# Which engine copies, how one weight is prepared, and when TensorE's work counts as ready, in a kernel of causal attention and a maxout layer

## Chip, cores and metric

The kernel runs on one core of a Trainium2 chip. The metric is the time of one execution in microseconds (us), taken on the device; lower is better.

## What is computed

```python
def _attn_ref(q, k, v):                    # (8, 8, 576, 64) float32
    scores = np.matmul(q, k.transpose(0, 1, 3, 2)) / np.sqrt(64)
    block = np.arange(576) // 64
    scores = np.where(block[:, None] >= block[None, :], scores, -1e9)
    scores = scores - np.max(scores, axis=-1, keepdims=True)
    attn = np.exp(scores)
    attn = attn / (np.sum(attn, axis=-1, keepdims=True) + 1e-09)
    return np.matmul(attn, v)

def _moe_ref(x, w1, w2, w3, w_out):        # w1..w3 (512, 768), w_out (768, 512)
    h = np.maximum(np.maximum(x @ w1, x @ w2), x @ w3)
    return h @ w_out

# out = _moe_ref(heads of the attention side by side: (4608, 512), w1, w2, w3, w_out)
```

Eight batches of eight heads, causal by blocks of 64 rows, and behind them, for each of the 4608 rows, the largest of three products and one more product.

## The kernel before

**Tiling.** Two heads of 64 make a pair, which fills 128 partitions; a batch has four pairs (`hp` 0 to 3). Of the 576 rows of a pair, 512 are worked in tiles of 128 queries, and the last 64 rows of both heads together as one tile more (`qk4`, `p4`). Products are taken in float32 accuracy from two parts of each number, a high one and a low one: high x high, high x low, low x high, which makes three matmuls of each product (a triplet).

**Stages of a pair.** Load K, Q, V; turn K and Q so that the head's 64 numbers lie on partitions; scores into banks of PSUM named `sb` (`qk` L1138 for batch 0, `block` L1020 for the whole pairs of later batches, `qk4` L1146 and L1150); row maximum on VectorE (L491), exponential on ScalarE (L675, P), sums, a scaling of P; P is turned; P times V on TensorE (`pv` L1212); the output is split into high and low parts (`xh`, `xl`).

**Batch 0 is done in a different way.** It is cut into the first 256 rows of all four pairs (FRONT) and the other 320 (BACK, `part.last`). K, Q and P are turned here by TensorE's transposes into `sb` banks (`raise_qk` L936 and L940, `raise4` L945 and L948, `raise_p` L631), from which ScalarE (L284) or VectorE (L286) copies them (`place_qk` for K and Q into `kq`; `place4` and `place` for P into `pt` or `pz`). For later batches VectorE turns 32x32 pieces and transfers put them in place.

**The layer.** Its work of the batch before stands between the attention steps on TensorE: `product` (L1381, into banks `pm`), the maximum (L1395), `project` (L1410).

**Weights.** The four matrices come in 24 units of 128x512. The units are prepared between 20 and 130 us: ScalarE takes an absolute value and the high part, VectorE has five steps (L379 to L401), and the remainder goes to TensorE, which adds it up in a `pm` bank for ScalarE to copy. [...]

**What sets the order.** Each step is a `Job` with a rank, costs on the engines that may do it, and what it needs. `in_order` plays the program with these costs: an engine that is free takes the ready job of the lowest rank whose buffers are free. Each engine's instructions are then issued in the order that comes out. A job that can go to ScalarE or VectorE goes to the one that is free first. Buffers count as slots: five `sb` banks, three `pm` banks, two tiles each of `pt` and `pz`. A job for TensorE whose last need was met by another engine (or by a transfer) counts as ready some time after that in the plan, if its rank is over 100 (from about 105 us on); a wait for a slot gets no such addition. At the start small matmuls without use (`spin`, L1444) keep TensorE at work.

Of the kernel before, what the change touches and what calls it, by code (L numbers as in the profile page):

```python
# [64 lines left out]
def in_order(jobs, slots):  # L65


    free = {}
    busy = {e: False for e in LAG}
    until = {"DVE": 0.0, "POOL": 0.0}  # L70
    ready = {e: [] for e in LAG}
    events, seq, out = [], 0, []
    moving = 0.0

    def post(t, kind, job, eng=None):
        nonlocal seq
        seq += 1
        heapq.heappush(events, (t, seq, kind, job, eng))

    def arrive(t, job, by=None):  # L80
        for e in job.cost:
            late = 250.0 if e == "PE" and by and by != "PE" and job.rank > 100.0 else 0.0
            post(t + late + (LAG[by][e] if by else 0.0), "ready", job, e)
        if not job.cost:
            post(landing(t, job), "done", job, "SP" if job.lasts else by)

    def landing(t, job):

        nonlocal moving
        t1 = t + job.lasts  # L90
        if job.moved:
            moving = max(moving, t) + job.moved
            t1 = max(t1, moving + DMA)
        return t1

    for n, job in enumerate(jobs):
        job.n, job.begun = n, False
        if job.left == 0:
            arrive(0.0, job)
    while events:  # L100
        t = events[0][0]
        while events and events[0][0] <= t:
            _, _, kind, job, eng = heapq.heappop(events)
            if kind == "ready":
                heapq.heappush(ready[eng], (job.rank, job.n))
            elif kind == "idle":
                busy[eng] = False
                for nxt in job.soon:
                    nxt.left -= 1
                    if nxt.left == 0:  # L110
                        arrive(t, nxt, eng)
            else:
                for s in job.give:
                    free[s] = free.get(s, slots[s]) + 1
                for nxt in job.next:
                    nxt.left -= 1
                    if nxt.left == 0:
                        arrive(t, nxt, eng)
        for eng, queue in ready.items():
            if busy[eng]:  # L120
                continue
            later = []
            while queue:
                top = heapq.heappop(queue)
                job = jobs[top[1]]
                if job.begun:
                    continue
                if all(free.get(s, slots[s]) >= job.take.count(s) for s in job.take):
                    for s in job.take:
                        free[s] = free.get(s, slots[s]) - 1  # L130
                    job.begun = busy[eng] = True
                    out.append((job, eng))
                    took = job.cost[eng]
                    if eng in job.alone:

                        took += max(0.0, until["POOL" if eng == "DVE" else "DVE"] - t)
                        until[eng] = t + took
                    post(t + took, "idle", job, eng)
                    post(max(t + took, landing(t, job)), "done", job, eng)
                    break  # L140
                later.append(top)
            for top in later:
                heapq.heappush(queue, top)
    assert all(j.begun or not j.cost for j in jobs), "no order"
    if DEBUG:
        print("model end", t, {e: sum(j.cost[g] for j, g in out if g == e) for e in LAG})
    return out
# [11 lines left out]
def act(n, psum=True):  # L159
    return (55.0 if psum else 95.0) + n / 1.2  # L160
# [7 lines left out]
def kernel(  # L168
# [30 lines left out]

    SECOND = 9  # L200
    NEAR = 4
    APART = 13
    XB = 3
    END = 40
    SPINS = 20
# [67 lines left out]

    def job(cost, rank, call, *args, after=(), take=(), give=(), lasts=0.0, moved=0.0, behind=None, alone=("POOL",)):
        j = Job(cost, rank, lambda eng: call(eng, *args), after, take, give, lasts, moved, behind, alone)
        jobs.append(j)
        return j

# [234 lines left out]
    class Head:  # L513
# [64 lines left out]
        def plain_turns(self, t0):  # L578
            pair, part = self.pair, self.pair.part
            heads = pair.heads  # L580
            shared = part.loads == 1 and self.j
            gate = heads[0].gate if shared else None
            first = heads[0].placed[0] if shared else None
            self.placed = []

            def place(call, *args, n, after):
                j = job(
                    {"ACT": act(n), "DVE": dve(n)} if part.last or pair.hp < 2 else {"ACT": act(n)},
                    t0 + 12,
                    call,  # L590
                    *args,
                    after=(after, first or (self.placed[0] if self.placed else None)),
                )
                self.placed.append(j)
                return j

            if part.last:
                if not self.j:
                    up = job({"PE": 4 * RAISE}, t0 + 11, pair.raise4, 0, after=(pair.scaled,), take=("sb", pair.tag, pair.tag))
                    pair.up4 = up, job({"PE": RAISE}, t0 + 11, pair.raise4, 1, after=(up,), take=("sb",))  # L600
                    join(pair.up4, ("p4",))
                gate = self.gate = pair.up4[0]
                for a, n in ((0, 256), (1, 64)):
                    place(self.place4, a, n=n, after=pair.up4[a])
                    if self.j:
                        join((self.placed[a], heads[0].placed[a]), ("sb",))

            for ts in [(t,) for t in part.tiles] if part.last else [part.tiles]:
                n = sum(ts) + len(ts)
                up = job(  # L610
                    {"PE": RAISE * n},
                    t0 + 12,
                    self.raise_p,
                    ts,
                    after=(*(self.scales[t] for t in ts), gate),
                    take=("sb",) if gate else ("sb", pair.tag),
                )
                gate = self.gate = gate or up
                join((up,), tuple(f"p{t}" for t in ts))
                join((place(self.place, ts, n=P * n, after=up),), ("sb",))  # L620
            self.moved = join(self.placed, ())
            self.first = None
            return None
# [92 lines left out]
    class Pair:  # L716
# [181 lines left out]
        def plain_qk(self, rank, loads):  # L898

            part, o = self.part, self.at // P  # L900
            banks = ((range(4), ((0, 0, 256),)),)
            if not self.apart:
                banks = (((o, o + 1, 4 + o, 5 + o), ((0, 1, 256), (256, 2, 256))),)
            if part.last:
                banks = ((2, 3, 8), ((0, 1, 256), (256, 0, 64))), ((4, 5, 6, 7), ((0, 2, 512),))
            ups, downs = [], []
            for n, (chunks, copies) in enumerate(banks):
                up = job(
                    {"PE": (2 * RAISE if self.apart else RAISE) * len(chunks)},
                    rank,  # L910
                    self.raise_qk,
                    n,
                    chunks,
                    after=(loads["kn"], loads["qn"]),
                    take=("sb", "sb5") + (("kq",) if n == 0 else ()),
                ) if n == 0 else job(
                    {"PE": RAISE * len(chunks)}, rank, self.raise_qk, n, chunks, after=(ups[0], loads["kn"], loads["qn"]), take=("sb", "sb5")
                )
                ups.append(up)
                put = []  # L920
                for c0, which, w in copies:
                    m = w if which else 2 * w
                    both = {"ACT": act(m), "DVE": dve(m)}
                    if not part.last:
                        both = {e: both[e] for e in (("ACT",) if which < 2 else ("DVE",))}
                    put.append(job(both, rank + 1, self.place_qk, n, c0, which, w, after=(up, *downs[:1]) if part.last else (up,)))
                    downs.append(put[-1])
                join(put, ("sb", "sb5"))
            join(ups, ("kn", "qn") * part.loads if not self.apart else (self.apart,))
            return join(downs, ())  # L930
# [588 lines left out]
```

## Time and profile before

| | us |
|---|---|
| Median of 3 runs (lowest to highest) | 859.13 (858.63 to 859.31) |
| The profiled execution's own time | 858.44 |
| Span of that execution in the trace | 856.7 |

| Engine | Busy, us | Share of span |
|---|---|---|
| TensorE, matmuls | 847.1 | 99% |
| TensorE, weight loads | 673.7 | 79% |
| VectorE | 521.0 | 61% |
| ScalarE | 467.4 | 55% |
| GpSimd | 292.6 | 34% |

The profiled execution took 1.74 us more than its span, and 0.69 us less than the median. PE is TensorE's matmuls, PEld its loading of weights (which runs beside them), DVE VectorE, ACT ScalarE, POOL GpSimd. Rows of a timeline give the start in us from the span's start, the time taken, and in brackets how long the engine was idle before and what ended it. Rows of one kind that follow each other are drawn together: `x20` is twenty instructions, and the time is from the first's start to the last's end, so a wait inside such a run lengthens it and doesn't appear as idle time.

### The profile page before, as it was taken

How to read it: one execution, taken by the hardware profiler on the slowest of the kernel's cores; microseconds unless marked ns; L12 is line 12 of the kernel's file. 1: busy time of each engine (PE TensorE's matmuls, PEld its weight loads, DVE VectorE, ACT ScalarE, POOL GpSimd, SP SyncE). 2: the span in 40 equal slices, each digit the busy share in tenths (PEclk: the TensorE clock that was granted, in tenths of full speed). 3: DMA queues.
4: the chain of work that ended last, by engine and by line, in shares of the span. 5: the costliest groups of instructions: out<-in, count | busy, mean ns of one | idle time of the engine just before them, and what ended most of it. 6: DMA issues, size and time to landing. Idle time of an engine off the chain costs nothing.

```text
span 856.7 us, 14921 instructions
## 1 busy us (share of the span) xinstructions
PE 847.1 (99%) x4866; PEld 673.7 (79%) x4866; DVE 521.0 (61%) x1540; ACT 467.4 (55%) x1305; POOL 292.6 (34%) x339
## 2 busy tenths in 40 slices
PE   8999999999999999999999999999999999999997
PEld 6677877788877788788878887888788778888886
DVE  6999998868782876568664866386638710110110
ACT  6997777667772765546573657465665422111111
POOL 3321113554453354514461345234443323110110
PEclk9999999999999999999999999999999999999999
DMA  8765348785777366745583558455655441001002
GB/s 239 216 191 142 69 96 190 140 186 100 164 162 171 62 138 146 160 105 112 111 191 77 112 117 180 110 120 121 132 143 108 93 116 63 0 1 50 0 1 50
DMA packets 240974, 100.36 MB, mean 117 GB/s; under 512 B 203008, under 2 KB 232704, under 8 KB 240896
## 3 DMA queue, kind: packets, MB, share of 16 engines
q1 hardware_dynamic: 236272, 86.42, 46.4%
q0 software_dynamic: 3456, 12.58, 4.6%
q8 instruction: 39, 0.64, 0.3%
q10 hardware_dynamic: 1168, 0.39, 0.2%
q14 instruction: 39, 0.32, 0.1%
HBM read 42.99 MB, written 10.49 MB: 62 GB/s over the span
## 4 chain that ended last, share of the span: by engine, by line
PE 91%; DVE 4%; ACT 3%; issue 1%; DMA 1%; SPq 0%; POOL 0%; ACTq 0%; DVEq 0%
PE pm L1381 51%; PE pm L1410 16%; PE pm L1212 7%; PE sb L1020 6%; PE sb L1150 2%; PE sb L1212 2%; ACT p L675 1%; DVE pz L698 1%; PE pm L414 1%; PE sb L1138 1%; DVE sb L491 1%; PE sb L631 1%; PE sb L1146 1%; PE sb L936 1%; PE pm L416 0%
## 5 line engine op out<-in xcount | busy, mean ns | idle before, releaser
L1381 PE MATMUL pm<-xh,w 128*128 128x512 f32 (+1 forms) x1296 | 386.4, 371 | 0.0
L1381 PEld LDWEIGHTS pm<-xh,w 128*128 128x128 f32 x1296 | 237.3, 188 | 45.1 <-issue 5.2
L1381 PE MATMUL pm<-xl,w 128*128 128x512 f32 (+1 forms) x648 | 237.3, 366 | 0.0
L675 ACT ACTIVATE p<-sb,nm 128x128 f32<-128x128 f32 (+3 forms) x256 | 133.7, 529 | 97.3 <-DVE nm L491 94.4
L1395 DVE TENSOR_TENSOR m<-pm,m 128x512 f32<-128x512 f32 (+1 forms) x120 | 74.5, 621 | 138.7 <-PE pm L1381 138.1
L698 DVE STREAM_TRANSPOSE pz<-p 128x512 f32<-128x512 f32 x280 | 133.6, 522 | 25.4 <-POOL p L511 11.3
L289 POOL TENSOR_TENSOR hl<-m,hh 128x512 fp32r<-128x512 f32 (+1 forms) x60 | 71.8, 1196 | 220.3 <-ACT hh L284 212.0
L491 DVE CUSTOM_DVE_ANT_1 sb<-sb,mask 128x256 f32<-128x256 f32 (+2 forms) x224 | 120.5, 566 | 37.0 <-PE sb L1150 34.9
L1381 PEld LDWEIGHTS pm<-xl,w 128*128 128x128 f32 x648 | 122.2, 189 | 19.2 <-issue 1.0
L1410 PE MATMUL pm<-wo,hh 128*128 128x512 f32 x432 | 134.1, 392 | 0.0
L289 POOL TENSOR_TENSOR kq<-kq 128x576 fp32r<-128x576 f32 x48 | 68.3, 1430 | 158.4 <-ACT kq L284 158.4
L511 POOL TENSOR_TENSOR p<-p,rs 128x512 f32<-128x512 f32 (+4 forms) x97 | 80.3, 853 | 101.8 <-DVE rs L852 65.2
L284 ACT CAST hh<-m 128x512 fp32r<-128x512 f32 (+1 forms) x60 | 34.6, 577 | 132.3 <-DVE m L1395 132.2
L284 ACT COPY m<-pm 128x512 f32<-128x512 f32 (+1 forms) x96 | 53.6, 559 | 93.2 <-PE pm L1410 63.5
L507 ACT ACTIVATE p<-p,rs 128x128 f32<-128x128 f32 (+4 forms) x176 | 89.3, 567 | 11.7 <-DVE rs L852 7.5
L1410 PEld LDWEIGHTS pm<-wo,hh 128*128 128x128 f32 x432 | 80.1, 188 | 16.8 <-issue 0.3
L1410 PE MATMUL pm<-wo,hl 128*128 128x512 f32 x216 | 84.2, 390 | 0.0
L1212 PE MATMUL pm<-pt,vn 128*64 128x320 f32 (+4 forms) x616 | 64.4, 360 | 0.0
L1212 PEld LDWEIGHTS pm<-pt,vn 128*64 128x64 f32 x616 | 38.5, 137 | 24.5 <-issue 1.4
L1020 PEld LDWEIGHTS sb<-kq 64*128 64x128 f32 x576 | 47.9, 185 | 8.7 <-issue 7.1
L1020 PE MATMUL sb<-kq 64*128 64x256 f32 (+3 forms) x576 | 53.1, 326 | 0.0
L675 ACT ACTIVATION_READ_ACCUMULATOR p<-sb,nm 128x1 f32 x256 | 51.5, 201 | 0.0
(129 smaller groups left out, 964.6 us busy)
## 6 DMA issues: line engine op xcount, KB each, us to landing
pt<-pz SPq DMA_DIRECT2D x224, 200.0 KB, 3.8
w<-in_moe_w_dram POOLq DMA_DIRECT2D x18, 512.0 KB, 5.5
vn<-in_v_dram SPq DMA_DIRECT2D x64, 128.0 KB, 3.5
out_dram<-m SPq DMA_DIRECT2D x32, 256.0 KB, 2.0
kq<-in_k_dram SPq DMA_DIRECT2D x112, 72.0 KB, 2.5
kq<-in_q_dram SPq DMA_DIRECT2D x112, 72.0 KB, 2.5
wo<-in_moe_w_out_dram POOLq DMA_DIRECT2D x6, 512.0 KB, 4.0
kq<-in_k_dram SPq DMA_DIRECT2D x8, 128.0 KB, 5.1
```

What stands on the lines that cost most here:

```text
L284: nc.scalar.copy(dst, src)
L289: {"DVE": nc.vector, "POOL": nc.gpsimd}[eng].tensor_tensor(out=dst, in0=a, in1=b, op=ALU.subtract)
L491: nc.vector.tensor_tensor_reduce(out=ps, in0=ps, in1=hidden, scale=-SCALE, scalar=first, op0=ALU.add, op1=ALU.min, accum_out=out_)
L507: nc.scalar.mul(p, p, r)
L511: nc.gpsimd.tensor_tensor(out=p, in0=p, in1=r.broadcast_to([P, p.shape[1]]), op=ALU.mult)
L675: nc.scalar.activation(dst, src, AF.Exp, bias=nm[:, c : c + 1], scale=-1.0, accum_out=sm[:, c : c + 1])
L698: nc.vector.transpose(dst, p[:, 0 : n * P])
L1020: nc.tensor.matmul(h.ps[t], qs[h.own, P * t : P * (t + 1)], ks[h.own, 0 : P * (t + 1)], start=(n == 0), stop=(n == 2),)
L1212: nc.tensor.matmul(o[h.own].rearrange("p (i u) -> p i u", u=n)[:, :, c0 : c0 + z - a], self.vn[own, kt, h.j, :], h.pt[own, :, h.off + a : ...
L1381: nc.tensor.matmul(self.ps, w[i, f][:, c, :], xx, start=(c == 0 and s == 0), stop=(c == NC - 1 and s == 2))
L1395: nc.vector.tensor_tensor(out=m, in0=ps, in1=m, op=ALU.max)
L1410: nc.tensor.matmul(self.po, h, w[f], start=(f == 0 and s == 0), stop=(f == NF - 1 and s == 2))
```

## The change

Five edits.

1. The time that TensorE's jobs count as ready later was 250 (ns in the plan) for all; now it is 700 for jobs `qk4`, `block` and `pv`, and 250 for the others.
2. `APART` is 12 instead of 13: unit number 12 (`w12`) has its remainder made by VectorE and takes two matmuls instead of three.
3. Turned P of BACK's pairs 2 and 3 is copied by ScalarE alone.
4. K and Q of BACK's pairs 2 and 3 are copied by ScalarE alone.
5. K and Q of FRONT's first two pairs are copied by one VectorE copy of 2x256 columns, instead of a ScalarE copy of 256 and a VectorE copy of 256.

```diff
     def arrive(t, job, by=None):
         for e in job.cost:
-            late = 250.0 if e == "PE" and by and by != "PE" and job.rank > 100.0 else 0.0
+            late = job.late if e == "PE" and by and by != "PE" and job.rank > 100.0 else 0.0
             post(t + late + (LAG[by][e] if by else 0.0), "ready", job, e)
...
-    APART = 13
+    APART = 12
...
         j = Job(cost, rank, lambda eng: call(eng, *args), after, take, give, lasts, moved, behind, alone)
+
+        j.late = 700.0 if call.__name__ in ("qk4", "block", "pv") else 250.0
         jobs.append(j)
...
-                    {"ACT": act(n), "DVE": dve(n)} if part.last or pair.hp < 2 else {"ACT": act(n)},
+                    {"ACT": act(n), "DVE": dve(n)} if pair.hp < 2 else {"ACT": act(n)},
...
             if not self.apart:
-                banks = (((o, o + 1, 4 + o, 5 + o), ((0, 1, 256), (256, 2, 256))),)
+                banks = (((o, o + 1, 4 + o, 5 + o), ((0, 0, 256),)),)
...
-                    both = {"ACT": act(m), "DVE": dve(m)}
+                    both = {"ACT": act(m), "DVE": dve(m)} if not part.last or self.hp < 2 else {"ACT": act(m)}
                     if not part.last:
-                        both = {e: both[e] for e in (("ACT",) if which < 2 else ("DVE",))}
+                        both = {e: both[e] for e in (("ACT",) if self.apart else ("DVE",))}
```

The changed kernel's lines from 276 on are numbered two higher. The transfers are the same in number. TensorE's order is the same up to about 60 us, differs from there to about 165 us, differs in small shifts of `product` against `block`, `qk4` and `pv` from 190 to 315 us, and is the same behind that. VectorE's remainders by L289 for weights go from 11 to 12.

Unit 12 on TensorE, about 63 us. Names: `pm` and `sb` are PSUM banks, `wo0` and `w12` the number and its low part, `plus` and `less` the unit matrix and its negative, `m` the small third part, `xh` and `xl` the attention's output. Before:

```order
L1138 MATMUL sb_982<-kq_833 128x384
L1138 MATMUL sb_983<-kq_833 128x384
L414 MATMUL pm_993<-wo0_758,plus_86 128x512
L415 MATMUL pm_993<-w12_986,less_88 128x512
L416 MATMUL pm_993<-m_966,plus_86 128x512
L1381 MATMUL pm_954<-xh_599,w5_666 128x256
L1381 MATMUL pm_954<-xl_600,w5_666 128x256
```

And in the changed kernel:

```order
L1214 MATMUL sb_998<-pt_892,vn_1_95 64x4x16
L1214 MATMUL sb_998<-pt_918,vn_1_95 64x4x16
L414 MATMUL pm_1026<-w12_985,plus_86 128x512
L418 MATMUL pm_1026<-m_982,plus_86 128x512
L414 MATMUL pm_1036<-w13_1009,plus_86 128x512
L418 MATMUL pm_1036<-m_991,plus_86 128x512
L1383 MATMUL pm_993<-xh_357,w6_683 128x256
```

The unit has two matmuls instead of three, and stands behind the P times V of the second pair, next to unit 13, where it stood behind the third pair's scores.

The ninth tile's scores of a pair of batch 2 on TensorE, at 279.61 us of the profile (`q8` and `less` hold the last rows' queries here). Before:

```order
L1381 MATMUL pm_3676<-xh_3552,w0_404 128x512
L1381 MATMUL pm_3676<-xl_3553,w0_404 128x512
L1381 MATMUL pm_3676<-xh_3552,w0_404 128x512
L1150 MATMUL sb_3704<-kq_3436,q8_2251 128x256 x2
L1150 MATMUL sb_3704<-kq_3436,less_2253 128x256
L1381 MATMUL pm_3710<-xh_3484,w1_458 128x512
L1381 MATMUL pm_3710<-xl_3485,w1_458 128x512
L1381 MATMUL pm_3710<-xh_3484,w1_458 128x512
L1381 MATMUL pm_3710<-xh_3488,w1_458 128x512
L1381 MATMUL pm_3710<-xl_3489,w1_458 128x512
L1381 MATMUL pm_3710<-xh_3488,w1_458 128x512
L1150 MATMUL sb_3728<-kq_3436,q8_2251 128x320 x2
```

And in the changed kernel:

```order
L1383 MATMUL pm_3695<-xh_3469,w1_456 128x512
L1383 MATMUL pm_3695<-xl_3470,w1_456 128x512
L1383 MATMUL pm_3695<-xh_3469,w1_456 128x512
L1383 MATMUL pm_3695<-xh_3474,w1_456 128x512
L1383 MATMUL pm_3695<-xl_3475,w1_456 128x512
L1383 MATMUL pm_3695<-xh_3474,w1_456 128x512
L1152 MATMUL sb_3713<-kq_3446,q8_2210 128x256 x2
L1152 MATMUL sb_3713<-kq_3446,less_2212 128x256
L1383 MATMUL pm_3695<-xh_3491,w1_456 128x512
L1383 MATMUL pm_3695<-xl_3492,w1_456 128x512
L1383 MATMUL pm_3695<-xh_3491,w1_456 128x512
L1152 MATMUL sb_3729<-kq_3446,q8_2210 128x320 x2
```

One triplet of products more stands ahead of the first half of `qk4` (five behind the pair's `block` instead of four), and one instead of two between its halves.

The K and Q copies of BACK's pair 2, on VectorE before (`rs4` and `sm4` belong to the ninth tile's sums, `wo4` and `w10` to weights):

```order
L1186 ISA rs4_750<-sm4_749,mask_79 128x2
L1186 ISA rs4_750 128x1
L286 COPY kq_833<-sb_820 128x256
L1199 RECIPROCAL rs4_750<-rs4_750 128x1
L379 TENSOR_SCALAR wo4_689<-wo4_689 128x512
L286 COPY kq_833<-sb_820 128x2x64
L286 COPY kq_833<-sb_825 128x512
L385 SCALAR_TENSOR_TENSOR wo4_689<-w10_543,wo4_689 128x512
```

And on ScalarE in the changed kernel:

```order
L286 CAST hh0_840<-m_637 128x256
L509 ACTIVATE p4_802<-p4_802,rs4_748 128x576
L286 COPY kq_851<-sb_818 128x256
L368 ACTIVATE wo1_854<-w13_645 128x512
L286 CAST w9_828<-pm_843 128x512
L286 COPY kq_851<-sb_818 128x2x64
L286 COPY kq_851<-sb_823 128x512
L368 ACTIVATE wo2_885<-w14_697 128x512
L286 COPY m_894<-pm_832 128x256
```

The three copies leave VectorE's row of weight steps and stand on ScalarE among weight copies and one scaling of P. Of the eight copies of pair 2's and the eight of pair 3's turned P, ScalarE had all but two of pair 2's before.

## Rows read from the trace of the kernel before

**Rows 1.** The page's busy time, share of the span and instructions of each engine, and its chain of work that ended last, by engine.

```profile
PE 847.1 (99%) x4866; PEld 673.7 (79%) x4866; DVE 521.0 (61%) x1540; ACT 467.4 (55%) x1305; POOL 292.6 (34%) x339
...
PE 91%; DVE 4%; ACT 3%; issue 1%; DMA 1%; SPq 0%; POOL 0%; ACTq 0%; DVEq 0%
```

**Rows 2.** Busy time by stretches: the stretch, its length, the busy us of PE, PEld, DVE, ACT and POOL (with their instructions), TensorE's granted clock, the busy share of the DMA engines, and GB/s.

```profile
24.00:51.00 27.00, 26.59 (x145) 16.31 (x145) 26.94 (x78) 26.43 (x69) 9.71 (x20) 1.00 0.74 211
51.00:74.00 23.00, 23.00 (x142) 16.94 (x141) 22.91 (x64) 20.00 (x48) 3.82 (x7) 1.00 0.55 155
74.00:104.00 30.00, 30.00 (x224) 25.42 (x223) 29.54 (x79) 23.69 (x62) 4.79 (x6) 1.00 0.43 99
104.00:128.00 24.00, 23.75 (x146) 18.12 (x145) 23.61 (x71) 19.31 (x53) 3.79 (x5) 1.00 0.46 91
128.00:170.00 42.00, 41.43 (x311) 32.51 (x312) 37.79 (x123) 29.56 (x93) 18.55 (x24) 1.00 0.77 168
170.00:315.00 145.00, 144.78 (x868) 115.58 (x866) 103.04 (x317) 90.06 (x266) 63.87 (x69) 1.00 0.66 139
```

**Rows 3.** Timeline of PE: unit 12, with three matmuls, and a later unit with two, each up to the next product.

```profile
63.33 1.02 PE L414 MATMUL pm<-wo,plus 128*128 128x512 f32 x2
63.79 0.79 PE L415 MATMUL pm<-w,less 128*128 128x512 f32 x1
64.42 0.39 PE L416 MATMUL pm<-m,plus 128*128 128x512 f32 x1
64.65 0.28 PE L1381 MATMUL pm<-xh,w 128*128 128x256 f32 x1
...
79.93 0.40 PE L412 MATMUL pm<-w,plus 128*128 128x512 f32 x1
80.16 0.40 PE L416 MATMUL pm<-m,plus 128*128 128x512 f32 x1
80.40 0.28 PE L1381 MATMUL pm<-xh,w 128*128 128x256 f32 x1
```

**Rows 4.** Timeline of PE: `pv` of 20 instructions at two places, its second half at one, and `pv` of 28 at two.

```profile
135.44 2.88 PE L1212 MATMUL sb<-pt,vn 128*64 128x320 f32 x20
138.82 0.87 PE L1212 MATMUL sb<-pt,vn 128*64 128x256 f32 x8 [0.50 <-ACT p L675]
151.19 2.28 PE L1212 MATMUL sb<-pt,vn 128*64 128x320 f32 x20
180.35 3.25 PE L1212 MATMUL sb<-pt,vn 128*64 128x320 f32 x28
243.26 2.93 PE L1212 MATMUL pm<-pt,vn 128*64 128x320 f32 x28
```

**Rows 5.** Timeline of PE: the last product ahead of the first half of `qk4` that the change's section shows, and that half.

```profile
279.02 0.39 PE L1381 MATMUL pm<-xh,w 128*128 128x512 f32 x1
279.61 0.51 PE L1150 MATMUL sb<-kq,q 128*128 128x256 f32 x2 [0.20 <-ACT p L675]
```

**Rows 6.** Timeline of PE: the scores of three whole pairs (`block`).

```profile
241.14 2.20 PE L1020 MATMUL sb<-kq 64*128 64x256 f32 x24
289.46 2.48 PE L1020 MATMUL sb<-kq 64*128 64x256 f32 x24
308.96 2.33 PE L1020 MATMUL sb<-kq 64*128 64x256 f32 x24
```

**Rows 7.** Timeline of the first pair of FRONT: its K and Q copies, the second pair's wait ahead of its scores' weights, and the first row maximum.

```profile
5.02 0.42 DVE L286 COPY kq<-sb 128x256 f32<-128x256 f32 x1 [3.10 <-PE sb L936]
5.47 0.37 ACT L284 COPY kq<-sb 128x256 f32<-128x256 f32 x1 [1.02 <-DVE kq L286]
...
7.60 0.52 PEld L1138 LDWEIGHTS sb<-kq 64*128 64x128 f32 x6 [0.24 <-ACT kq L284]
7.70 0.43 DVE L491 CUSTOM_DVE_ANT_1 sb<-sb,mask 128x256 f32<-128x256 f32 x1 [0.56 <-PE sb L1138]
```

**Rows 8.** Groups of instructions by line and shape: copies out of `sb` banks by VectorE (L286) and ScalarE (L284). Behind the count: busy us in all, mean ns of one, idle us before them and what ended it.

```profile
L286 DVE COPY kq<-sb 128x256 f32<-128x256 f32 x6 | 2.5, 422 | 4.4 <-PE sb L936 4.4
L286 DVE COPY kq<-sb 128x512 f32<-128x512 f32 x3 | 2.0, 676 | 0.0
L286 DVE COPY kq<-sb 128x128 f32<-128x128 f32 x4 | 1.1, 279 | 0.0
L284 ACT COPY kq<-sb 128x512 f32<-128x512 f32 x3 | 1.8, 594 | 0.0
L284 ACT COPY pt<-sb 128x512 f32<-128x512 f32 x3 | 1.8, 587 | 0.0
L284 ACT COPY pt<-sb 128x384 f32<-128x384 f32 x5 | 2.6, 513 | 0.0
L284 ACT COPY pt<-sb 128x256 f32<-128x256 f32 x3 | 1.0, 375 | 0.4 <-PE sb L948 0.4
L284 ACT COPY pt<-sb 64x64 f32<-64x64 f32 x4 | 0.7, 209 | 0.0
```

**Rows 9.** VectorE's remainders of weights (L289): least, mean and longest ns, when, and shape; and GpSimd's timeline about the one that took longest.

```profile
L289 DVE TENSOR_TENSOR w<-wo,w x5: 677/680/685, 68.6 to 87.8; 128x512 fp32r<-128x512 f32 x5
L289 DVE TENSOR_TENSOR wo<-pz,wo x1: 1168/1168/1168, 121.8 to 121.8; 128x512 fp32r<-128x512 f32 x1
...
119.88 2.50 POOL L511 TENSOR_TENSOR p<-p,rs 128x384 f32<-128x384 f32 x3 [10.12 <-DVE rs L848]
```

## The prediction

> **What bounds the kernel now.** I read the page first, for who is busy and who ends the chain: TensorE's matmuls fill 847.1 of 856.7 us, and 91% of the chain that ended last is TensorE's own work [rows 1]. Then the table by stretches, which tells where anything else could set the pace. [...] From 51 to 104 us TensorE has no idle time; 24 to 51 has 0.41 us of it (27.00 - 26.59), 104 to 128 has 0.25, 128 to 170 has 0.57, and 170 to 315 has 0.22 [rows 2]. VectorE is just as full while the weights are prepared (22.91 of 23.00, 29.54 of 30.00), and ScalarE has 9.31 us to spare between 51 and 104 (53.00 - 20.00 - 23.69) [rows 2]. So the kernel is TensorE's list of matmuls plus small waits, and an edit is worth what it takes off that list and out of those waits; an edit to a copy is worth something only if TensorE then waits less, or more. Third come the timelines of TensorE at the places of the change, since a wait inside a run of matmuls is no idle time in the table: there I compare a run with another of the same kind.
>
> **Unit 12 (APART 12).** The unit with three matmuls takes TensorE from 63.33 to the next product at 64.65, 1.32 us; the unit with two takes from 79.93 to 80.40, 0.47 us [rows 3]. TensorE is never idle there, so all of the difference is on the path: -0.85 us. VectorE gets one remainder more, 0.68 us as five of its like take [rows 9], in a stretch where it has hardly a gap. That cover is not VectorE's spare time but the copies that leave it in the same stretch, below.
>
> **K, Q and P of the last two pairs to ScalarE.** VectorE loses per pair a copy of 256, one of 128 and one of 512 columns of K and Q: 0.42 + 0.28 + 0.68 = 1.38 us, 2.76 us for two pairs [rows 8]. Less the remainder, it is freed of 2.1 us. ScalarE gains 0.37 + 0.28 + 0.59 = 1.24 us per pair, 2.5 us in all; its copy of 128 columns is in no row, lies between 0.21 (64x64) and 0.375 (128x256), and is taken as VectorE's 0.28 [rows 8]. The two copies of P that change sides are of the same size on either, and ScalarE had the other fourteen already. Of ScalarE's 9.31 us of spare time 6.8 are left [rows 2]. So the sum of either engine's work fits; what it does to TensorE is only through when a bank of `sb` comes free and when K and Q are ready, and I put it into the last term below. If the cover goes, the price is the slower rival's.
>
> **First two pairs (one copy for two).** Before, VectorE copies at 5.02 for 0.42 us, and ScalarE at 5.47 for 0.37 us, having waited for VectorE [rows 7]: both are done at 5.84. One copy of 512 columns takes 0.68 us [rows 8] and would be done at 5.70. That is 0.14 us, and only one wait hangs on it: the weights of the second pair's scores, 0.24 us [rows 7]. The first row maximum at 7.70 waits for the first pair's scores and not for a copy. Between 0 and -0.14 I take 0, since the row maximum begins the chain that the start waits for.
>
> **Margin of 700 for `pv`.** The `pv` at 135.44 takes 2.88 us, where twenty such instructions at 151.19 take 2.28: 0.60 us of waiting inside the run. The one at 180.35 takes 3.25 against 2.93 for twenty-eight at 243.26: 0.32 us [rows 4]. Both need P from transfers, so the margin applies, and it grows by 0.45 us (700 - 250). In the plan TensorE then takes products first and comes to `pv` later by up to that much: -0.45 of the 0.60 and all of the 0.32, -0.77 us. The products that go ahead are not extra work, only earlier.
>
> **Margin for `qk4`.** Products follow each other 0.23 us apart (79.93, 80.16, 80.40) [rows 3]. `qk4` starts 0.59 us behind the product at 279.02 [rows 5], which is 0.36 us of waiting. In the changed order one triplet more stands ahead of it, three matmuls of 0.23 us, which is more than the wait. So -0.36 us, and this one I read from the order, whatever the cause of the move.
>
> **Margin for `block`.** The usual block takes 2.20 us; the one at 289.46 takes 2.48 and the one at 308.96 takes 2.33 [rows 6]: 0.28 + 0.13. Their wait is for the low parts of K and Q by GpSimd, which the margin reaches: -0.41 us. Further blocks behind 315 us are in the same order as before and count nothing.
>
> **The new order from 51 to 170 us.** All edits together reorder TensorE here, and what it waits for in a new order no row shows. At best the idle time that is there now goes, 0.25 + 0.57 = 0.82 us [rows 2] (0.50 of it is the second half of `pv` at 138.82, waiting for a bank that an exponential empties [rows 4]). At worst the stretch gets waits as densely as the nearest busy one, 24 to 51 us: 0.41 in 27 us makes 1.81 us in 119 us, 0.99 more than now. I take +0.5, nearer to the worse end, because VectorE from 51 to 104 is as full as it is in that stretch, and ScalarE moves toward being so [rows 2].
>
> **The sum.** -0.85 - 0.77 - 0.36 - 0.41 + 0.5 = -1.89 us. The span goes from 856.7 to 854.8 and the profiled execution's own time from 858.44 to 856.5. That execution was 0.69 us under the median of the runs shown, so on the median 859.13 becomes 857.2 us, -0.22%. I use 0.2% of the time, 1.72 us, as what a measurement can tell from no change: faster is below 857.4, slower above 860.85.
>
> **Rivals.**
>
> *The margin does nothing.* It moves a job's ready time in a plan, and not a wait for a bank: the wait at 138.82 and the one ahead of `qk4` end on an exponential that gives a bank back [rows 4, 5], which has no margin. The plan's durations may also differ from the chip's by more than 0.45 us at 135 and 180 us. Then `pv` and `block` keep their waits: -0.85 - 0.36 + 0.5 = -0.71, 858.4 us. For it: two of the waits named are on banks. Against: `pv` and `block` wait for transfers and GpSimd. Chance 0.24.
>
> *All of the waits go.* Behind 0.45 us of margin stand whole triplets of 0.68 us (3 x 0.23), so a `pv` that is put behind one more triplet is later by more than its wait: -0.92 for `pv` in place of -0.77, and if the stretch from 51 to 170 also loses its 0.82: -0.85 - 0.92 - 0.36 - 0.41 - 0.82 = -3.36, 855.8 us. For it: VectorE is freed of 2.1 us just there. Chance 0.17.
>
> *Slower: ScalarE alone empties the banks too slowly.* TensorE's transposes of the last two pairs need `sb` banks, and ScalarE has exponentials and weight copies in the same row (the third fence of the change). If its three K and Q copies come one after the other before TensorE can take the scores, and then one head's four copies of P before it can take `pv`, TensorE waits per pair 1.24 + (0.375 + 0.21 + 0.59 + 0.51 = 1.68) = 2.92 us [rows 8], 5.84 for two. With the other terms that is 859.13 - 1.89 + 5.84 = 863.1 us. It makes the kernel slower by over 0.2% from about 3.6 us of new waits (1.89 + 1.72). Against: the 6.8 us that ScalarE has left, other work of TensorE (products of the front chunk) between a pair's copies and its scores, and no idle time of TensorE from 51 to 104 us now [rows 2]. Chance 0.07.
>
> *TensorE's list isn't the bound.* The busy share has modelled ends; weight loads are busy 79% [rows 1]. If something else set the pace, the terms would change nothing: 859.1 us. Against it, matmuls start 0.23 us apart without a gap [rows 3]. Chance 0.04. [...]
>
> *The remainder is slowed by GpSimd.* One remainder of the same shape took 1.17 us at 121.8, while GpSimd was at the scaling of P from 119.88 to 122.38; the other five took 0.68 [rows 9]. If the new one falls beside such work it costs VectorE 0.49 us more, and if all of that came through to TensorE: 857.7 us. Chance 0.03. [...]
>
> **How the numbers follow.** The forecast's own case has 0.45, 857.2 give or take 0.6; a little over half of it (0.27) lies below 857.4. The margin without effect (0.24), TensorE not the bound (0.04) and GpSimd (0.03) lie within 0.2%, with the other 0.18 of the forecast: same 0.49. All of the waits (0.17) and the 0.27: faster 0.44. Slower 0.07. For the range: from the case in which all of the waits go, 855.8, to the one in which unit 12 alone pays and the new order is at its worst, -0.85 + 0.99 = +0.14, 859.3.
>
> **What would show it.** Right: unit 12 takes about 0.47 us of TensorE; `pv` near 135 and 180 takes 2.3 and 2.9 to 3.0; `block` takes 2.1 to 2.2 everywhere up to 315 us; `qk4` near 279 has no wait; from 51 to 170 us TensorE is idle for 0.8 to 1.8 us; ScalarE is busier by some 2.5 us from 51 to 104, and VectorE shows a gap or two there. Wrong: waits of TensorE on ScalarE's copies of `kq`, `pt` or `pz` from 60 to 120 us (the slower rival), or `pv` and `block` as long as before (the margin without effect), or shorter waits that come back as others further down, so that the span doesn't follow the sum.

## The result, and the profile after

| | before | after |
|---|---|---|
| Median, us (lowest to highest, 6 runs each) | 859.04 (857.69 to 859.31) | 865.24 (864.23 to 866.53) |
| Ratio after/before, 95% interval | | 1.0076 (1.0066 to 1.0086) |
| Span of the profiled execution, us | 856.7 | 863.3 |

The changed kernel is slower by 6.2 us; the forecast was 857.2, its range ended at 859.3. I begin as with the kernel before, with the table by stretches (the columns of [rows 2]):

```profile
51.00:74.00 23.00, 23.00 (x143) 17.08 (x143) 22.78 (x62) 18.90 (x47) 7.13 (x7) 1.00 0.49 140
74.00:104.00 30.00, 29.91 (x223) 25.16 (x223) 29.50 (x78) 26.02 (x70) 3.82 (x6) 1.00 0.44 110
104.00:128.00 24.00, 23.92 (x143) 17.90 (x143) 23.71 (x73) 19.36 (x54) 5.54 (x7) 1.00 0.50 101
128.00:170.00 42.00, 41.10 (x309) 32.07 (x309) 37.50 (x121) 29.45 (x93) 18.22 (x24) 1.00 0.76 163
170.00:315.00 145.00, 139.71 (x809) 111.30 (x806) 98.20 (x298) 86.89 (x255) 58.95 (x64) 0.99 0.63 134
```

Where the edits to copies and weights lie, 51 to 170 us, TensorE is idle for 1.07 us in all (0.09 + 0.08 + 0.90), against 0.82 before. The loss is in the stretch that I had taken as quiet: 170 to 315 us has 5.29 us of idle time, against 0.22 [rows 2], and a granted clock under 1.00. TensorE's own waits (line, what it waited for, us in total, times, longest) name two places:

```profile
PE sb L1152 <- ACT p L677: 3.6, 1, 3.6
PE pm L1383 <- POOL xl L291: 1.0, 1, 1.0
...
PE pm L1383 <- ACT xh L286: 0.7, 1, 0.7
```

The first is at 287 us, the other two are at 187 to 189 us. The same block of scores shows how the delay grows: the first whole pair's starts at 169.38 before and at 169.67 after, the one that starts at 328.70 before starts at 335.70 after. (The 0.29 us are made of a start 0.50 us later, unit 12's gain of 0.75 and 0.54 us lost on the way. The first transposes waited 0.89 us for Q from memory in this execution, 0.39 before and 0.60 in e11. On the way there is a new wait of 0.48 us for a bank ahead of `qk4`, at 154.82.)

**The place at 283 to 290 us.** Timelines of TensorE, of ScalarE, of VectorE, and of SyncE's queue (SPq, the issuing of transfers) in the changed kernel:

```profile
283.14 0.39 PE L1383 MATMUL pm<-xh,w 128*128 128x512 f32 x1
287.12 0.75 PE L1152 MATMUL sb<-kq,q 128*128 128x256 f32 x2 [3.59 <-ACT p L677]
```

```profile
286.29 0.69 ACT L677 ACTIVATE p<-sb,nm 128x512 f32<-128x512 f32 x1
```

```profile
284.17 1.38 DVE L1122 STREAM_TRANSPOSE kq<-kq 128x1152 f32<-128x1152 f32 x1 [5.50 <-DMA kq<-in_q_dram]
285.48 0.67 DVE L493 CUSTOM_DVE_ANT_1 sb<-sb,mask 128x512 f32<-128x512 f32 x1
```

```profile
265.59 1.96 SPq L1081 DMA_DIRECT2D kq<-in_k_dram  x4
267.65 7.12 SPq L714 DMA_DIRECT2D pt<-pz  x8
...
279.90 2.02 SPq L1081 DMA_DIRECT2D kq<-in_q_dram  x4
```

This is how to read them together. TensorE waits for a bank that an exponential gives back (L677). The exponential waits for a row maximum (L493). The row maximum could have started when the scores were done, at 279.89 (block at 277.70, 2.19 us), but VectorE runs it at 285.48, since ahead of it in VectorE's order stands the turning of K and Q of the pair after (L1122), and that waits 5.50 us for a load of Q. The load was issued at 279.90: behind the K load of that pair, eight moves of turned P (7.12 us of issuing alone) and the transfers of results, of held-back rows and of V, with no pause over 0.33 us between these rows of the queue (265.59 to 279.90). Before, the same three rows were

```profile
257.23 2.11 SPq L1079 DMA_DIRECT2D kq<-in_k_dram  x4
259.86 6.68 SPq L712 DMA_DIRECT2D pt<-pz  x8
...
272.21 2.11 SPq L1079 DMA_DIRECT2D kq<-in_q_dram  x4
```

7.7 us earlier, while the block that the load runs against stood only 3.4 us earlier (274.26 before, 277.70 after). The K load was later because the buffer it takes is given back by GpSimd's low part of the pair before (it ends at 257.21 before and at 265.56 after, and K is issued at 257.23 and 265.59). GpSimd had that pair's two low parts next to each other before; in the new order two scalings of P and four subtractions for other work stand between them. The rows before, and in the changed kernel:

```profile
254.38 2.83 POOL L289 TENSOR_TENSOR kq<-kq 128x576 fp32r<-128x576 f32 x2
```

```profile
256.81 1.44 POOL L291 TENSOR_TENSOR kq<-kq 128x576 fp32r<-128x576 f32 x1 [8.87 <-ACT kq L286]
...
264.16 1.40 POOL L291 TENSOR_TENSOR kq<-kq 128x576 fp32r<-128x576 f32 x1
```

This was read from the order and the traces and not tried by itself. The other traces bear it out: the starts of the two low parts lie 6 to 8 us apart in every kernel below that has the wait near 285 us (e1, e7, e8, e12), and 1.3 to 1.4 us apart in e2, e6, e9, e10 and e11, which don't have it. (In e3, e4 and e5 they are apart too, and there the turning or Q's load is moved.)

In all, finished scores waited 5.6 us behind the turning (279.89 to 285.48): 4.28 us until it could start, in which VectorE did nothing else, and 1.31 us from its start to the row maximum's.

**What the wait costs on top.** The same stretch by windows (columns as in [rows 2]):

```profile
284.00:287.00 3.00, 0.00 (x0) 0.00 (x0) 2.83 (x8) 1.38 (x4) 0.66 (x1) 1.00 0.00 1
287.00:288.00 1.00, 0.88 (x4) 0.88 (x5) 1.00 (x7) 1.00 (x5) 0.74 (x1) 0.60 0.02 8
288.00:290.00 2.00, 2.00 (x8) 1.71 (x8) 1.51 (x8) 2.00 (x10) 0.00 (x0) 0.50 0.00 0
290.00:291.00 1.00, 1.00 (x5) 0.82 (x5) 0.62 (x2) 0.30 (x3) 0.00 (x0) 0.69 0.00 0
```

Behind the idle time the granted clock is 0.60, 0.50 and 0.69 in the three windows from 287 to 291 us, and 1.00 in the windows next to them: as much as 0.50 for about 3 us. From 287.12 to 290.39 TensorE does both halves of `qk4` and four products. In the kernel before, at a granted clock of 1.00 (every window from 279 to 283 us), these take 0.46 + 0.44 (the halves at 279.61 and 281.43, each to the next product) and 4 x 0.23 us, 1.82 us; here they took 3.27. So the place costs 3.59 + 1.45 = 5.0 us.

**The place at 185 to 190 us.** Again a turning waits for a Q load, for 2.29 us, and here the queues of VectorE, ScalarE and GpSimd carry the delay on:

```profile
184.29 1.38 DVE L1122 STREAM_TRANSPOSE kq<-kq 128x1152 f32<-128x1152 f32 x1 [2.29 <-DMA kq<-in_q_dram]
...
186.19 0.78 DVE L288 COPY x<-sb 128x320 f32<-128x320 f32 x2
```

```profile
185.76 1.25 ACT L286 CAST kq<-kq 128x576 fp32r<-128x576 f32 x2 [2.15 <-DVE kq L1122]
187.01 0.62 ACT L286 CAST xh<-x 128x512 fp32r<-128x512 f32 x1
```

```profile
187.68 0.50 PE L1383 MATMUL pm<-xh,w 128*128 128x512 f32 x1 [0.66 <-ACT xh L286]
189.21 0.50 PE L1383 MATMUL pm<-xl,w 128*128 128x512 f32 x1 [1.03 <-POOL xl L291]
```

ScalarE splits K and Q of the turned pair ahead of the attention's output (`xh`) that TensorE's products wait for. That order alone isn't it: the copies of the output that `xh` needs (`x`) are on VectorE behind the turning and end at 186.97, so `xh` could not have started earlier either. Before, Q was issued as late (at 180.09; in the changed kernel at 179.91) and the turning waited too (1.17 us), but the copies of `x` were on ScalarE (from 183.23) with `xh` behind them (184.04), ahead of K and Q, and TensorE did not wait.

### The profile page after: what moved, and what is told of

Its sections match the earlier page's. It is cut to its first block, busy times and chain, and to the rows that moved or that the text cites. A ratio compares the mean times of both kernels' runs of the same rounds, so it can differ in the third digit from the quotient of the medians.

```text
span 863.3 us, 14914 instructions
## 1 busy us (share of the span) xinstructions
PE 848.3 (98%) x4864; PEld 673.6 (78%) x4864; DVE 522.7 (61%) x1538; ACT 467.7 (54%) x1308; POOL 293.3 (34%) x337
## 4 chain that ended last, share of the span: by engine, by line
PE 87%; ACT 4%; SPq 3%; DMA 2%; DVE 2%; issue 1%; POOL 1%; ACTq 0%; DVEq 0%; POOLq 0%
PE pm L1383 50%; PE pm L1412 14%; PE pm L1214 7%; PE sb L1022 6%; PE sb L1152 2%; PE sb L1214 2%; SPq L714 2%; ACT p L677 2%; PE sb L1140 1%; DMA kq<-in_q_dram 1%; PE pm L416 1%; PE sb L633 1%; PE sb L1148 1%; SPq L1081 1%; DMA pt<-pz 0%
## 5 line engine op out<-in xcount | busy, mean ns | idle before, releaser
L677 ACT ACTIVATE p<-sb,nm 128x128 f32<-128x128 f32 (+3 forms) x256 | 133.7, 529 | 104.5 <-DVE nm L493 101.0
L700 DVE STREAM_TRANSPOSE pz<-p 128x512 f32<-128x512 f32 (+1 forms) x280 | 134.2, 523 | 26.6 <-POOL p L513 10.8
L493 DVE CUSTOM_DVE_ANT_1 sb<-sb,mask 128x256 f32<-128x256 f32 (+2 forms) x224 | 120.7, 568 | 37.7 <-PE sb L1152 34.7
L286 ACT CAST hh<-m 128x512 fp32r<-128x512 f32 (+1 forms) x60 | 34.6, 577 | 128.8 <-DVE m L1397 128.8
L286 ACT COPY m<-pm 128x512 f32<-128x512 f32 (+1 forms) x96 | 53.6, 558 | 93.6 <-PE pm L1412 63.4
L509 ACT ACTIVATE p<-p,rs 128x512 f32<-128x512 f32 (+4 forms) x177 | 90.1, 567 | 10.6 <-DVE rs L854 7.2
L1022 PE MATMUL sb<-kq 64*128 64x384 f32 (+3 forms) x576 | 52.7, 325 | 0.0
L677 ACT ACTIVATION_READ_ACCUMULATOR p<-sb,nm 128x1 f32 x256 | 51.6, 201 | 0.0
```

Source lines behind the costliest of these rows:

```text
L286: nc.scalar.copy(dst, src)
L493: nc.vector.tensor_tensor_reduce(out=ps, in0=ps, in1=hidden, scale=-SCALE, scalar=first, op0=ALU.add, op1=ALU.min, accum_out=out_)
L509: nc.scalar.mul(p, p, r)
L677: nc.scalar.activation(dst, src, AF.Exp, bias=nm[:, c : c + 1], scale=-1.0, accum_out=sm[:, c : c + 1])
L700: nc.vector.transpose(dst, p[:, 0 : n * P])
L1022: nc.tensor.matmul(h.ps[t], qs[h.own, P * t : P * (t + 1)], ks[h.own, 0 : P * (t + 1)], start=(n == 0), stop=(n == 2),)
```

## The experiments

All ratios are to the kernel before, run beside them on the same chip (858.49 us for e1 to e4, 858.99 for e5 to e8, 858.58 for e9 to e12). Theory Q: TensorE's waits come from jobs that stand in an engine's order behind a turning whose Q load SyncE issues late. Theory M: the margin of 700 does it.

**e1, the margin undone.**

```diff
-            late = job.late if e == "PE" and by and by != "PE" and job.rank > 100.0 else 0.0
+            late = 250.0 if e == "PE" and by and by != "PE" and job.rank > 100.0 else 0.0
```

> The changed kernel with the margin of 250 for all jobs (edit 1 undone, edits 2 to 5 kept). Theory Q (a late load): the 3.6 us that TensorE waits ahead of qk4 near 283 us come from VectorE, whose turning of the pair after next stands ahead of the row maxima and waits for a Q load that the SyncE queue issues behind eight moves of P; the margin is not what does it, so the wait stays, 864 to 866 us. Theory M (the margin): block, pv and qk4 come later by the margin of 700 and drag the transfers with them; without it the wait goes, 858 to 860 us.

865.37 us, 1.0078 (1.0059 to 1.0098). Theory M falls. The wait is there again, ahead of the second half of `qk4` instead of the first (2.61 us).

**e2, APART undone.**

```diff
-    APART = 12
+    APART = 13
```

> The changed kernel with APART 13 (edit 2 undone, the others kept, the margin of 700 too). Theory Q: in this order the Q load of the pair that waits is issued some 4 us earlier against the turning; the wait near 283 us goes, the third matmul group of unit 12 comes back (+0.85): 859.5 to 861.5 us. Theory M: the margin is still there, so the wait stays: 865 to 866 us.

860.38 us, 1.0024 (1.0014 to 1.0034). The wait near 283 us is gone, with the margin still there; the one near 187 us is not (1.3 + 0.9 us).

**e3, one turning moved.** Here no edit of the change is undone.

```diff
-                    after=(loads["kn"], loads["qn"]),
+                    after=(loads["kn"], loads["qn"], *([h.tops for h in before.heads] if (self.b, self.hp) == (3, 2) else ())),
```

(`tops` is the last row maximum of a head.)

> The changed kernel with one job moved: VectorE turns K and Q of pair 2 of batch 3 behind the row maxima of pair 1 instead of ahead of them; the loads stay where they are. Theory Q: the row maxima no longer stand behind the load, TensorE's wait of 3.6 us and the low clock behind it (about 1.4 us) go: 859.5 to 861 us. Theory M: no change, 864.5 to 866 us.

859.63 us, 1.0012 (1.0002 to 1.0021): by the two ratios (1.0076 and 1.0012) some 5.5 us less than the changed kernel, by one VectorE job put behind the row maxima. The plan follows it: SyncE's order stays as it was, and that of the other engines up to about 280 us; behind that the first half of `qk4` stands two triplets earlier and other work shifts. VectorE runs the turning at 284.32 with no wait ahead of it, and `qk4` of TensorE follows its products:

```profile
281.45 0.40 PE L1153 MATMUL sb<-kq,q 128*128 128x256 f32 x2
...
282.50 0.45 PE L1153 MATMUL sb<-kq,q 128*128 128x320 f32 x2
```

```profile
284.32 1.38 DVE L1123 STREAM_TRANSPOSE kq<-kq 128x1152 f32<-128x1152 f32 x1
```

The load was nearly as late (Q issued at 278.72; 279.90 in the changed kernel): it is not the late load that costs, it is what stands behind it.

**e4, Q's load right behind K's.**

```diff
-                        after=(loads.get("kn"),)
+                        behind=loads.get("kn"),
+                        after=()
                         if loads
```

> The changed kernel with the loads of Q for whole pairs issued right behind those of K, and no longer ready only when K has landed. Theory Q: the Q load is issued some 10 us earlier near 280 us and earlier near 180 us too; both waits (5 us near 283 to 290, 2.2 us near 185 to 190) go: 857 to 859.5 us. Theory M: 864.5 to 866 us. Against both: the moves of P come about 2 us later in the queue and pv may wait for them.

864.68 us, 1.007 (1.0055 to 1.0085). A miss. Q of the pair in question is issued at 260.95 and its wait near 283 us is gone, but the place near 187 us is as late as ever (Q issued at 179.92) and costs more, and five small waits come at other `qk4`:

```profile
PE sb L1153 <- ACT p L677: 1.9, 5, 1.0
PE pm L1384 <- POOL xl L291: 1.7, 1, 1.7
...
PE pm L1384 <- ACT xh L286: 0.8, 1, 0.8
```

The edit also reorders the queues far behind this place. To issue a load early is no cure by itself.

**e5, two turnings moved.** e3's line, with `before.before.outs` for pair (2, 1) in place of `()`: the copies of the attention's output that stood behind its turning.

```diff
+... if (self.b, self.hp) == (3, 2) else before.before.outs if (self.b, self.hp) == (2, 1) else ())),
```

> The changed kernel with two jobs moved: the turning of pair 2 of batch 3 behind the row maxima of pair 1 (as in e3), and the turning of pair 1 of batch 2 behind the copies of the attention's output of batch 1's last pair. Theory Q (jobs that stand in order behind a turning that waits for a late Q load): e3's 859.6 us loses the 2.3 to 2.9 us near 185 to 190 us too, 856.5 to 858 us, so that the forecast's own terms (-1.9 us) are seen. Rival D (the waits move on to the next place of the new order): 859 to 861 us.

856.63 us, 0.9975 (0.9965 to 0.9985). Faster than both kernels. ScalarE now has `xh` ahead of K and Q, and nothing on TensorE waits there:

```profile
184.40 0.62 ACT L286 CAST xh<-x 128x512 fp32r<-128x512 f32 x1
...
186.94 1.25 ACT L286 CAST kq<-kq 128x576 fp32r<-128x576 f32 x2 [1.43 <-DVE kq L1124]
```

**e6, Q planned to land later.** One number of the plan, no job named.

```diff
-                        lasts=n * LOAD + DMA,
+                        lasts=n * LOAD + DMA + (3000 if loads else 0.0),
```

> The changed kernel with one number of the plan changed: for whole pairs the plan takes Q to land 3 us later than it did, so that all turnings are planned later against the load. No job is touched by hand. Theory Q: both waits go, 856.5 to 859 us. Rival D: turnings come later for all pairs, blocks wait for K and Q: over 861 us.

856.92 us, 0.9977 (0.9966 to 0.9987). Over the whole span VectorE waits for Q loads about as long as in the changed kernel (there 11.2 us, longest 5.5), but elsewhere:

```profile
DVE kq L1122 <- DMA kq<-in_q_dram: 11.1, 3, 3.9
```

The three waits end at 451, 541 and 631 us, and TensorE has no idle time near any of them: nothing that it needs soon stands behind them. From 170 to 330 us VectorE waits for no Q, and TensorE has no idle time.

**e7, e8, e12: three of the edits, each alone on the kernel before.** e7 is `APART = 12`, e8 the two lines on ScalarE's copies (edits 3 and 4), e12 the margin of 700 for `qk4`, `block` and `pv`.

> The kernel before with APART 12 alone (edit 2). Theory T (the edits' own terms add up): the unit's 0.85 us, 857.6 to 858.5 us. Theory Q: the plan's slack between the landing of Q and the turning for pair 2 of batch 3 falls from 3.7 us to 0.2 us with this edit alone too, so the unit's gain comes with waits near 185 and 285 us: 861 to 865 us.

> The kernel before with the copies of the last two pairs by ScalarE alone (edits 3 and 4). Theory T: within 0.2% of the kernel before, 857.5 to 860 us. Theory S (the slower rival of the prediction: ScalarE empties the banks too slowly): new waits of TensorE between 55 and 125 us, 860 to 863 us. Theory Q: no waits there, but the plan's slack for pair 2 of batch 3 falls from 3.7 us to 0.1 us, and the waits come near 185 and 285 us: 861 to 865 us.

> The kernel before with the margin of 700 alone (edit 1). By the prediction's terms (pv 0.77, block 0.41, qk4 0.36): 857.2 to 858 us. Theory Q: with this edit alone too the plan leaves the turning of pair 2 of batch 3 only 0.1 us behind the landing of Q (3.7 us before), so waits come near 285 us: 860.5 to 865 us.

e7 867.48 us, 1.0095 (1.0076 to 1.0115), and e12 865.42 us, 1.007 (1.005 to 1.009), both over what I expected, e7 by 2.5 us; e8 864.03 us, 1.0054 (1.0034 to 1.0075). Any of the three is enough to bring the wait at the same pair, whichever half of `qk4` it meets:

```profile
287.39 0.72 PE L1150 MATMUL sb<-kq,q 128*128 128x256 f32 x2 [3.66 <-ACT p L675]
```

```profile
286.02 0.79 PE L1150 MATMUL sb<-kq,q 128*128 128x320 f32 x2 [3.13 <-ACT p L675]
```

```profile
287.58 0.90 PE L1151 MATMUL sb<-kq,q 128*128 128x320 f32 x2 [2.85 <-ACT p L676]
```

(of e7, e8 and e12). The place near 185 us, which I had expected in e7 and e8 too, has waits in neither. Theory T, by which the edits' terms add up, falls; so does theory S for e8: between 55 and 125 us TensorE was idle for 0.35 us, 0.25 before.

**e9, e10, e11: what is left when no load holds TensorE up.** e9 is e6 with e1's line, e10 is e6's line on the kernel before, e11 is edit 5 alone on the kernel before.

> As e6 (Q planned to land 3 us later), but with the margin of 250 for all jobs. What is the margin of 700 worth once the late loads hold nothing up? By the prediction's terms (block 0.41, pv 0.77) it is 1.2 us: 857.5 to 858.5 us beside e6's 856.9. Rival: the waits inside block and pv go with the order and not with the margin: 856.5 to 857.3 us.

> The kernel before with Q planned to land 3 us later, nothing else. Theory Q: no load holds up TensorE in that kernel, so nothing is to be had: 858 to 860 us. Rival: the later turnings alone are worth the 2 us that e6 shows against the kernel before: 856.5 to 857.5 us.

> The kernel before with one VectorE copy of K and Q for the first two pairs (edit 5). Every other instruction stays in its place, so this is the edit's own worth: within 0.2 us, 858.4 to 859.4 us. By another reading ScalarE's copy beside VectorE's was worth something: 0.3 us more, 859.3 us and over.

e9 857.30 us, 0.9987 (0.9978 to 0.9997): at the upper end of what the rival allowed, and its interval overlaps e6's, so a worth of the margin is not told from nothing. e10 858.02 us, 0.9992 (0.9982 to 1.0001): no change that can be told. e11 858.57 us, 1.0001 (0.9991 to 1.001): edit 5 is worth nothing, as forecast.

**The plan's own numbers beside the times.** For pair 2 of batch 3, how long the plan lets Q land ahead of the start of its turning (the planned start of the turning less that of the load, less the 4.28 us that the kernel before plans for the load and 0.1 us from engine to engine), and the measured median (the kernel before, run beside each, took 858.5 to 859.0):

```
kernel   plan: Q lands ahead by   measured
before   3.7 us                   859.0
e11      3.7                      858.6
e2       3.7                      860.4
e3       4.4                      859.6
e5       4.3                      856.6
e6       3.0                      856.9
e9       3.0                      857.3
e10      3.0                      858.0
after    0.0                      865.2
e1       0.2                      865.4
e7       0.2                      867.5
e8       0.1                      864.0
e12      0.1                      865.4
```

On the chip this stretch of SyncE's queue takes longer than in the plan (eight moves of P 7.12 us against 8 x 620 ns planned), so a slack of nothing can become waiting; the moves make up some 2.2 of the 5.5 us, and the rest was not followed. 3.7 us were enough: before, the turning ran at 276.66, when the scores ahead of it were done, and Q, issued at 272.21, came in time. The slack says nothing by itself. The same working gives 0.0 us for five other pairs of the kernel before (pairs 2 and 3 of batch 2 among them), where TensorE has no such wait, and 0.85 us for this pair in e4, which lost its wait here.

## Why the prediction was wrong

**The step that failed** is "The new order from 51 to 170 us". In that stretch the term was about right: 0.25 us more idle time, where +0.5 was taken. But it bounded what TensorE waits for in a new order by 0.99 us, and only up to 170 us; the stretch behind it, where the orders differ "in small shifts", was given gains and no loss. There the runs show 5.07 us more idle time of TensorE, and 1.45 us more for work at a granted clock of 0.50 to 0.69, for which the prediction's sum had no term. The shifts of TensorE's products were small there. What moved far was on other engines: GpSimd's second low part behind six other jobs, and with it K's load, eight moves of P and Q's load on SyncE. The prediction's last sign of being wrong, "shorter waits that come back as others further down", comes nearest, but it had neither a price nor a chance. I followed each moved copy to its engine, but not the queues of VectorE, ScalarE, GpSimd and SyncE at the places where TensorE would later need a bank. Each of edits 1, 2 and 3 with 4 alone does it (e12, e7, e8).

**Unit 12:** right. In the changed kernel it takes 0.57 us to the next unit (0.47 forecast, against 1.32 before), for a gain of 0.75:

```profile
71.01 0.50 PE L414 MATMUL pm<-w,plus 128*128 128x512 f32 x1
71.34 0.39 PE L418 MATMUL pm<-m,plus 128*128 128x512 f32 x1
71.58 0.39 PE L414 MATMUL pm<-w,plus 128*128 128x512 f32 x1
```

**ScalarE alone:** right that it holds nothing up where it works. The amounts were off: from 51 to 104 us ScalarE is busier by 1.2 us (44.92 against 43.69) and not by 2.5, and VectorE is freed of 0.2 us (52.27 against 52.45), not 2.1. The slower rival was the right sign with the wrong mechanism: no wait of TensorE from 60 to 120 us was for such a copy. **First two pairs:** right (e11).

**Margin for `pv`:** wrong. The `pv` at 135 us takes 2.99 us in the changed kernel (2.88 before), and 3.09 in e5; the one at 181 takes 3.45 there and 2.93 in e5. In e1 and e9, with the margin of 250, the latter takes 2.93 too, so its wait goes and comes with the order of the rest.

**Margin for `block`:** the size was right, the reason was not. All blocks up to 315 us take 2.2 us in the changed kernel and in e5; but they do in e7, e8, e9 and e10 as well, without the larger margin.

**Margin for `qk4`:** wrong at the very place that I showed. One triplet more stands ahead of it, as the order said, and the idle time ahead of it went from 0.20 to 3.59 us, because the release of its bank moved by more. A cover that is read from one engine's order holds only if the releaser stays where it is.

**The sum:** with the two turnings out of the way (e5) the change is worth 2.4 us (858.99 to 856.63), near the 1.9 forecast; but of its terms only unit 12 (0.75) is tied to its edit. The `block`, `qk4` and second `pv` terms show in e5 as well (2.19, no wait, 2.93 us), as properties of that order. They show in e10 too (2.19, no wait, 2.93 us), which has none of the five edits. And with the loads out of the way in both, e6 against e10, the change is worth some 1.3 us by the two ratios (0.9977 and 0.9992), whose intervals overlap: a gain of 1.9 us was neither confirmed nor ruled out. That e5 came near it does not confirm the forecast's terms.

**Left open:** which single decision of the plan puts GpSimd's low part behind the six others with each of the three edits, and what the other 2 us of e7 over the changed kernel are made of in detail (one wait of 2.0 us for a bank at `pv` is among them).

## What to carry to other kernels

When a change moves work in a scheduler's order, look past the engine that sets the time: at each place where it waits for a buffer, follow the releaser back through its own queue to the transfer at the far end, and compare that transfer's place in its queue before and after. What an engine's wait for a load costs here hung on what stood behind it in the same queue: the 5.50 us near 284 us in the changed kernel cost TensorE 3.59 us of idle time, since a row maximum stood there that it needed; the 11.1 us of e6 cost it none. Where a plan lets a load land just in time, an edit that has nothing to do with it can break it (three of the four tried alone did); a few microseconds of planned slack (e6) took the waits out without touching a job, and an edit's worth can be measured only with that done.

## What the runs showed of the hardware

In some of these executions the granted clock made such a wait dearer, and not in proportion to it. In the profiled execution of e1 TensorE stood idle for 2.61 us and the granted clock stayed at 1.00. In that of e12 it was idle for 2.85 us, and 0.50 stood in every window from 287 to 293 us:

```profile
287.00:288.00 1.00, 0.42 (x1) 0.42 (x2) 1.00 (x4) 1.00 (x7) 0.52 (x1) 0.50 0.00 0
...
292.00:293.00 1.00, 1.00 (x4) 0.81 (x3) 0.68 (x2) 0.31 (x2) 0.66 (x2) 0.50 0.00 0
```

Behind the 3.59 us of the changed kernel it was at 0.50 for about 3 us only. The same kernel differs in this from one execution to the next: e1's profiled execution took 863.13 us at a mean granted clock of 0.999, its other three 865.04 to 867.39 us at 0.995 to 0.997; e12 took 862.23 us at 0.999 and otherwise 865.37 to 866.15 us at 0.995 to 0.997. So what the clock adds to such a wait is not read from one trace.
